# Waits of TensorE at the matmuls that need them, and thirteen opening matmuls less, in a scan with adapters behind it

## The chip, the cores and the metric

The kernel runs on one core of a Trainium2 chip. The metric is the device time of one execution in microseconds, the median of several runs. Profiles are taken from one further execution; their times count from the start of its span.

## The reference

```python
h = zeros((8, 128))
for t in range(6400):                     # for each of 8 sequences
    h = a[:, t] * h + b[:, t]             # a, b: (8, 6400, 128), f32
    x[:, t] = h
x = x.reshape(51200, 128)
logits = x @ w_gate                       # 128 -> 8 experts
top 2 of 8, softmax over the two: w
delta = sum over the two of w * ((x @ A[e]) @ B[e])    # rank 16
out = x + delta                           # (51200, 128), f32
```

The kernel reads a and b once (52.6 MB) and writes the output once (26.2 MB).

## The kernel before, in words

The 51,200 tokens are cut into 100 chunks of 512. Tokens lie on partitions when they are loaded (`a_tm`, `b_tm`, four slots of four chunks each) and have to stand along the free axis for the scan, so each chunk goes through these steps:

- Loads. `x` (a, four chunks, 1 MB) and `y` (b, two chunks, 512 KB) are issued by SyncE's queue (SP) and wait until TensorE has read the old contents of the slot.
- Transposes on TensorE (line 306, against `ident_f`) into PSUM. Chunks at the beginning and the end are done alone (`a`, `b`: four matmuls of 128x128). All others are fused (`f`, line 403): sixteen matmuls, in which eight of a's, for a chunk some way ahead, alternate with eight of b's, on the two halves of the rows. b goes to banks 1 and 2 in turn (`BANK_B`), which the scan frees; all other operations of TensorE take the six banks of `RING` in turn, which the copy out of the bank frees.
- a is copied to `a_st` by ScalarE (`a`, line 342); VectorE runs the scan (`s`, line 358) with a from SBUF and b from PSUM, and writes `xT`.
- `z` (line 455): up to three blocks of 128 tokens times the eight adapters' A and the gate, 136 columns each; ScalarE copies the result to `zl` (line 462).
- The gating of a group (six chunks in the middle, one or two at the ends), in small operations `1` to `8`, `p`, `q`, `r`, `u` on VectorE, GpSimd and ScalarE, lines 487 to 520.
- `m` (line 544): zl times gate, on GpSimd or VectorE; `t` (line 552): transposes of the product, for one or two chunks; a copy to `zwT` on ScalarE or VectorE (line 561).
- `d` (lines 579 and 580): for each of four blocks, the block of `xT` times the identity, then `zwT` times B on top of it. ScalarE copies to `outt` (`o`, line 587), SP stores (line 616), one or two chunks at a time.

Each engine does its operations in the order that the strings of `ORDER` spell, letter by letter (line 24 on). `Program.arrange` lays them out, `banks` gives the PSUM banks out in TensorE's order and adds a dependence on the copy that frees each, and `waits` walks through all five orders and finds which semaphore counts an operation has to wait for that its engine does not know of already. `run` (line 663) issues all waits of an operation ahead of its first instruction. The last instruction of an operation raises the engine's semaphore by one. SP's string mixes loads and stores in one order, so a store that waits holds back the loads behind it.

At the beginning `w` (line 262) transposes the identity into the last bank of the ring: `WARM` = 14 times, five before the first data, the others between the first chunks' operations. Nothing reads the results.

Of the kernel before, what the change touches and what calls it, by code (L numbers as in the profile page):

```python
# [58 lines left out]


class Op:
    __slots__ = ("i", "eng", "kind", "deps", "emit", "sem", "cnt", "clock", "dur", "alt", "lock", "size", "pos", "ring", "rows")


class Bank:


    __slots__ = ("n", "evac")


class Program:
# [4 lines left out]
    def __init__(self):  # L76
        self.ops = []
        self.at = 0.0

    def add(self, eng, kind, deps, emit, sem=None, dur=0.0, lock=False, alt=None, size=0, ring=None, rows=0):  # L80
# [8 lines left out]
        op.rows = rows  # L89
        self.ops.append(op)  # L90
        return op

# [18 lines left out]
    def banks(self, ring):  # L111

        turns = []
        for op in self.order["pe"]:
            if op.ring is not None:
                op.ring.n = ring[len(turns) % len(ring)]
                assert len(turns) < len(ring) - 1 or not any(o.kind == "w" for o in self.order["pe"][self.order["pe"].index(op) :])
                if len(turns) >= len(ring):
                    op.deps.append(turns[-len(ring)].evac)
                turns.append(op.ring)  # L120

    def waits(self):
        landed = {}
        out = {}
        known = {e: {} for e in self.ENGINES}
        at = {e: 0 for e in self.ENGINES}
        left = len(self.ops)
        while left:
            moved = False
            for e in self.ENGINES:  # L130
                while at[e] < len(self.order[e]):
                    op = self.order[e][at[e]]
                    if any(d.clock is None for d in op.deps):
                        break
                    k = known[e]
                    need = {}
                    for d in sorted(op.deps, key=lambda d: -d.i):
                        if d.sem is None and d.eng == e == "pe":
                            continue
                        key = d.eng if d.sem is None else d.sem  # L140
                        if k.get(key, 0) < d.cnt:
                            need[key] = max(need.get(key, 0), d.cnt)
                            for kk, v in d.clock.items():
                                k[kk] = max(k.get(kk, 0), v)
                            k[key] = max(k.get(key, 0), d.cnt)
# [12 lines left out]
def bass_associative_scan_2x2__then__mixture_of_adapters_kernel(  # L158
# [21 lines left out]
    span = {}  # L180
# [7 lines left out]
    with ExitStack() as stack:  # L188
# [41 lines left out]
        P = Program()  # L230
        eng = {}
# [4 lines left out]
        s_eng = {e: sem("s_" + e) for e in ("pe", "act", "dve", "pool")}  # L236
        s_dma = {}
# [23 lines left out]
        for k in range(WARM):  # L261
            w = P.add("pe", "w", [o_id], lambda: eng["pe"].transpose(ps[:, RING[-1], 0:128], ident_f[:, :], ident_f[:, :]),
                      dur=0.212)
# [7 lines left out]
        o_la, o_lb, place = {}, {}, [{}, {}]  # L271
# [114 lines left out]
        def front(c):  # L386
            P.at = c
            bb = Bank()
            bb.n = bank_b(c)
            sl, q, m, h = place[0][c]  # L390
            if m == 1:
                solo_a(c, 0)
            elif (c - h, 0) not in o_A:
                for p in (0, 2):
                    for g in (0, 1):
                        solo_a(c - h + p, g)
            deps, ts = turned(1, c, bb)
# [39 lines left out]
        def scanned(b):  # L437
            c0, m = span[b // 4]
            return o_sc[c0 + m - 1]
# [7 lines left out]
        def zlogits(b0, n):  # L447
            P.at = (b0 + n - 1) / 4
            bk = Bank()
            z0 = zpos[b0]  # L450
            assert n <= 3

            def zmm():
                for k in range(n):
                    last = eng["pe"].matmul(ps[:, bk.n, k * W : k * W + W], xblock(b0 + k), Awg_h)  # L455
                return last

            o = P.add("pe", "z", [scanned(b0 + n - 1), o_ch], zmm, dur=(0.059 if span[b0 // 4][1] == 1 else 0.062) * n, ring=bk)
            for k in range(n):
                reads(b0 + k, o)  # L460
            z = P.add("act", "z", [o] + [z_user[z0 + k] for k in range(n)],
                      lambda: eng["act"].copy(  # L462
                          zl[:, z0 : z0 + n, :].rearrange("p k w -> p (k w)"), ps[:, bk.n, 0 : n * W]),
                      dur=0.145 + 0.1172 * n)
            bk.evac = z
            for k in range(n):
                o_ze[b0 + k] = z
                z_user[z0 + k] = z
# [59 lines left out]
        def back(gi, c0, q0, n):  # L528
# [41 lines left out]
        def out_chunk(c, e_t):  # L570
# [9 lines left out]
                    last = eng["pe"].matmul(dst, zwT[:, w, k * 128 : k * 128 + 128], B_h, start=False, stop=True)  # L580
# [82 lines left out]
        def run(name, handle):  # L663
            eng[name] = handle
            for op in P.order[name]:
                for key, v in waits[op.i]:
                    handle.wait_ge(s_eng[key] if key in s_eng else s_dma[key], v)
# [18 lines left out]

        @block.tensor
        def _(pe):
            run("pe", pe)

        @block.scalar
        def _(act):
# [2 lines left out]
        @block.vector  # L695
        def _(dve):
            run("dve", dve)


class Unordered(Exception):  # L700
# [29 lines left out]
```

## Time and profile before

| | |
|---|---|
| Median of 3 runs | 203.28 us (203.12 to 203.54) |
| Profiled execution | 203.03 us, of which the span is 201.2 |
| Granted TensorE clock, mean | 0.987 |
| Busy: PE, DVE, ACT, POOL | 179.9, 177.1, 178.2, 127.4 us |
| DMA | 79.28 MB, mean 394 GB/s |
| Matmuls | 3150 |

PE is TensorE's matrix part, PEld its loading of weights, DVE VectorE, ACT ScalarE, POOL GpSimd, SP SyncE. The queue of an engine is marked with a q. L306 is line 306 of the kernel, the one before. "Issue" is time for which the profile shows no reason. Durations of TensorE's matmuls overlap: the distance of two starts tells the pace, not the duration.

### The profile page before, as it was taken

How to read it: one execution, taken by the hardware profiler on the slowest of the kernel's cores; microseconds unless marked ns; L12 is line 12 of the kernel's file. 1: busy time of each engine (PE TensorE's matmuls, PEld its weight loads, DVE VectorE, ACT ScalarE, POOL GpSimd, SP SyncE). 2: the span in 40 equal slices, each digit the busy share in tenths (PEclk: the TensorE clock that was granted, in tenths of full speed). 3: DMA queues.
4: the chain of work that ended last, by engine and by line, in shares of the span. 5: the costliest groups of instructions: out<-in, count | busy, mean ns of one | idle time of the engine just before them, and what ended most of it. 6: DMA issues, size and time to landing. Idle time of an engine off the chain costs nothing.

```text
span 201.2 us, 7662 instructions
## 1 busy us (share of the span) xinstructions
PE 179.9 (89%) x3150; PEld 164.3 (82%) x3150; DVE 177.1 (88%) x269; ACT 178.2 (89%) x384; POOL 127.4 (63%) x205
## 2 busy tenths in 40 slices
PE   4986788899989998999999999899999999898880
PEld 3975676788989998899999998789989898897760
DVE  0587689999989998999999999898999999999860
ACT  2376597999999999999999999899999999999970
POOL 1024006692797979785998697678788885865420
PEclk9999699999999999999999999999999999999998
DMA  6999999999999999999999999999999999998596
GB/s 189 396 410 414 414 410 412 416 421 396 419 415 419 409 411 423 410 423 406 419 418 405 418 415 415 416 415 414 422 410 411 415 407 404 418 360 346 234 357 226
DMA packets 21379, 79.28 MB, mean 394 GB/s; under 512 B 3424, under 2 KB 3552, under 8 KB 18400
## 3 DMA queue, kind: packets, MB, share of 16 engines
q1 hardware_dynamic: 19872, 78.39, 96.5%
q10 hardware_dynamic: 1472, 0.40, 0.9%
q8 instruction: 25, 0.41, 0.9%
q14 instruction: 10, 0.08, 0.1%
HBM read 52.56 MB, written 26.21 MB: 391 GB/s over the span
## 4 chain that ended last, share of the span: by engine, by line
PE 51%; DVE 17%; DMA 16%; ACT 5%; issue 4%; SPq 3%; POOL 2%; ACTq 0%
PE ps L306 20%; DMA b_tm<-in_b_dram 16%; DVE xT L358 10%; PE ps L455 10%; PE ps L579 8%; PE ps L552 7%; PE ps L580 6%; DVE zw L544 3%; ACT outt L587 3%; SPq L291 3%; ACT zl L462 1%; DVE zwT L561 1%; POOL g L518 1%; DVE L L492 1%; DVE k L490 0%
## 5 line engine op out<-in xcount | busy, mean ns | idle before, releaser
L358 DVE TENSOR_TENSOR_SCAN xT<-a_st,xT,ps 128x512 f16<-128x512 f32 x96 | 120.2, 1253 | 7.4 <-PE ps L306 5.3
L544 POOL TENSOR_TENSOR zw<-zl,g 128x512 f16<-128x512 f32 x82 | 85.9, 1069 | 9.9 <-PE ps L552 8.6
L306 PE MATMUL ps<-ident_f,a_tm 64*128 64x64 f32 (+1 forms) x768 | 66.3, 232 | 6.6 <-DVE xT L358 2.4
L462 ACT COPY zl<-ps 128x408 f32<-128x408 f32 (+1 forms) x138 | 67.9, 596 | 4.7 <-PE ps L455 4.5
L342 ACT COPY a_st<-ps 128x512 f32<-128x512 f32 x100 | 62.9, 691 | 7.3 <-PE ps L306 6.9
L306 PE MATMUL ps<-ident_f,b_tm 64*128 64x64 f32 (+1 forms) x768 | 66.0, 233 | 2.8 <-DMA b_tm<-in_b_dram 1.5
L306 PEld LDWEIGHTS ps<-ident_f,a_tm 64*128 64x128 f32 (+1 forms) x768 | 55.9, 141 | 13.0 <-issue 3.0
L587 ACT COPY outt<-ps 128x512 f32<-128x512 f32 x100 | 61.5, 691 | 2.9 <-PE ps L580 2.3
L306 PEld LDWEIGHTS ps<-ident_f,b_tm 64*128 64x128 f32 (+1 forms) x768 | 54.9, 141 | 4.4 <-issue 2.4
L579 PE MATMUL ps<-ident_h,xT 128*128 128x128 f16 x400 | 57.3, 231 | 0.6 <-ACT zwT L561 0.4
L580 PE MATMUL ps<-cst_h,zwT 128*128 128x128 f16 x400 | 55.7, 220 | 1.7 <-issue 1.7
L579 PEld LDWEIGHTS ps<-ident_h,xT 128*128 128x128 f16 x400 | 49.5, 142 | 3.9 <-ACT zwT L561 0.9
L580 PEld LDWEIGHTS ps<-cst_h,zwT 128*128 128x128 f16 x400 | 42.7, 107 | 1.1 <-issue 1.1
L455 PE MATMUL ps<-cst_h,xT 128*128 128x136 f16 x400 | 41.7, 232 | 1.3 <-DVE xT L358 0.9
L455 PEld LDWEIGHTS ps<-cst_h,xT 128*128 128x128 f16 x400 | 32.2, 145 | 4.2 <-DVE xT L358 1.4
L552 PE MATMUL ps<-ident_h,zw 128*128 128x128 f16 x400 | 30.8, 219 | 1.4 <-DVE k L490 0.6
L552 PEld LDWEIGHTS ps<-ident_h,zw 128*128 128x128 f16 x400 | 23.9, 98 | 3.3 <-ACT outt L587 0.8
L561 ACT COPY zwT<-ps 128x1024 f16<-128x1024 f16 (+1 forms) x21 | 21.7, 1033 | 0.0
L561 DVE COPY zwT<-ps 128x1024 f16<-128x1024 f16 (+1 forms) x31 | 20.3, 658 | 1.2 <-PE ps L552 1.2
L518 POOL TENSOR_TENSOR g<-k,w 128x192 f32<-128x192 f32 (+3 forms) x23 | 10.7, 467 | 11.4 <-DVE k L503 9.5
L498 POOL TENSOR_TENSOR dd<-m 128x24 f32<-128x24 f32 (+3 forms) x23 | 5.8, 251 | 16.5 <-DVE m L496 16.5
L501 POOL TENSOR_TENSOR dd<-m 128x24 f32<-128x24 f32 (+3 forms) x23 | 6.0, 259 | 15.1 <-DVE m L496 15.0
(23 smaller groups left out, 90.2 us busy)
## 6 DMA issues: line engine op xcount, KB each, us to landing
a_tm<-in_a_dram SPq DMA_DIRECT2D x23, 1024.0 KB, 16.4
b_tm<-in_b_dram SPq DMA_DIRECT2D x46, 512.0 KB, 16.8
out_dram<-outt SPq DMA_DIRECT2D x46, 512.0 KB, 14.4
a_tm<-in_a_dram SPq DMA_DIRECT2D x8, 256.0 KB, 9.7
out_dram<-outt SPq DMA_DIRECT2D x8, 256.0 KB, 5.2
b_tm<-in_b_dram SPq DMA_DIRECT2D x7, 256.0 KB, 11.8
b_tm<-in_b_dram ACTq DMA_DIRECT2D x1, 256.0 KB, 3.6
cst_f<-in_moe_A_dram ACTq DMA_DIRECT2D x1, 64.0 KB, 4.3
```

The costliest lines, as they stand in the source:

```text
L306: return [lambda k=k: eng["pe"].transpose(dv(k), src[r, 8 * g + k, :], ident_f[r, r]) for k in range(n)]
L342: lambda: eng["act"].copy(dst, src()), dur=AE[0 if m == 1 else 1])
L358: last = eng["dve"].tensor_tensor_scan(out=xT[:, xb, s0:s1], data0=a_st[:, c % NA, s0:s1], data1=ps[:, bk, s0:s1], initial=init, op0=ALU.m ...
L455: last = eng["pe"].matmul(ps[:, bk.n, k * W : k * W + W], xblock(b0 + k), Awg_h)
L462: lambda: eng["act"].copy(zl[:, z0 : z0 + n, :].rearrange("p k w -> p (k w)"), ps[:, bk.n, 0 : n * W]),
L518: lambda: eng["pool"].tensor_tensor(out=gg, in0=kk2, in1=bc(u2), op=ALU.mult), dur=pd)
L544: lambda me=me, wv=wv, zv=zv, gv=gv: eng[me].tensor_tensor(out=wv, in0=zv, in1=gv, op=ALU.mult),
L552: last = eng["pe"].transpose(ps[:, bt.n, :].bitcast(F16)[:, k * 128 : k * 128 + 128], zw[:, w + k // 4, k % 4, :], ident_h[:, :])
L561: f = (lambda: eng["act"].copy(dst, src())) if te == "act" else (lambda: eng["dve"].tensor_copy(dst, src()))
L579: eng["pe"].matmul(dst, xblock(b0 + k), ident_h[:, :], start=True, stop=False)
L580: last = eng["pe"].matmul(dst, zwT[:, w, k * 128 : k * 128 + 128], B_h, start=False, stop=True)
L587: lambda: eng["act"].copy(outt[:, p0 : p0 + 4, :].rearrange("p k d -> p (k d)"), ps[:, bo.n, :]), dur=0.6)
```

## The change

`WARM` goes from 14 to 1, and the thirteen letters `w` go from TensorE's string; nothing else in any order changes. All else concerns where TensorE waits. An operation now knows the number of its matmuls (`mm`) and which of its dependences only a later matmul needs (`late`: a place and the dependences). In `f` that is the second matmul, for all but a's load and the ring's bank; in `d` the second, for the copy `zwT` and for B; in `t` the fifth, for the product of the second chunk. Then `lend` goes through TensorE's order: where an operation would still wait for two or more semaphores ahead of its first matmul, one of them, a DMA's if there is one, is waited for at the last matmul of the operation before it, as long as the wait does not depend on that operation itself and the orders still run through. A wrapper around the engine counts the matmuls of an operation and puts each wait ahead of the one it belongs to. In the built programs 501 matmuls of the new one wait for one semaphore and 46 for two; before, 216 waited for one, 105 for two, 22 for three and 19 for four.

```diff
-WARM = 14
+WARM = 1
...
-        "wwwwwbawwabwzzwwwwbwwazzbaaaazzaztffffzztzfdzzffzzfdfzfzzzffzzftzzffdzfdzzftzfzfzdfdzfzzzfzzfttzzffd"
+        "wbaabzzbazzbaaaazzaztffffzztzfdzzffzzfdfzfzzzffzzftzzffdzfdzzftzfzfzdfdzfzzzfzzfttzzffd"
...
                 if len(turns) >= len(ring):
-                    op.deps.append(turns[-len(ring)].evac)
+                    evac = turns[-len(ring)].evac
+                    op.deps.append(evac)
+                    op.late = (op.late[0], [d for d in op.late[1] if d is not evac])
...
+    def lend(self):
+
+        waits = self.waits()
+        pe = self.order["pe"]
+        for prev, op in zip(pe, pe[1:]):
+            need = dict(waits[op.i][0][1])
+            last = prev.mm - 1
+            if len(need) < 2 or last < 1 or prev.tail or last == prev.late[0]:
+                continue
+            for key in sorted(need, key=lambda k: k in self.ENGINES):
+                moved = [d for d in op.deps if (d.eng if d.sem is None else d.sem) == key and d is not prev]
+                if any(self.reaches(d, prev) for d in moved):
+                    continue
+                prev.tail = moved
+                try:
+                    self.waits()
+                    break
+                except AssertionError:
+                    prev.tail = []
...
-                    need = {}
-                    for d in sorted(op.deps, key=lambda d: -d.i):
...
-                    out[op.i] = list(need.items())
+                    out[op.i] = []
+                    for place, part in ((0, [d for d in op.deps if d not in op.late[1]]), op.late, (op.mm - 1, op.tail)):
+                        need = {}
+                        for d in sorted(part, key=lambda d: -d.i):
...
+                        out[op.i].append((place, list(need.items())))
...
-                o = P.add("pe", "f", deps + deps2, each(ts2, ts), dur=FUSED[2], lock=True, ring=ba)
+                o = P.add("pe", "f", deps + deps2, each(ts2, ts), dur=FUSED[2], lock=True, ring=ba, mm=16, late=(1, [d for d in deps if d is not o_id]))
...
-            o = P.add("pe", "z", [scanned(b0 + n - 1), o_ch], zmm, dur=(0.059 if span[b0 // 4][1] == 1 else 0.062) * n, ring=bk)
+            o = P.add("pe", "z", [scanned(b0 + n - 1), o_ch], zmm, dur=(0.059 if span[b0 // 4][1] == 1 else 0.062) * n, ring=bk, mm=n)
...
-            o_t = P.add("pe", "t", o_mu + [o_ih], tr, dur=0.224 * n, ring=bt)
+            o_t = P.add("pe", "t", o_mu + [o_ih], tr, dur=0.224 * n, ring=bt, mm=4 * n, late=(4, o_mu[1:]))
...
-            o_D[c] = P.add("pe", "d", [e_t, o_cB], delta, dur=0.448 if span[c][1] == 1 else 0.48, ring=bo)
+            o_D[c] = P.add("pe", "d", [e_t, o_cB], delta, dur=0.448 if span[c][1] == 1 else 0.48, ring=bo, mm=8, late=(1, [e_t, o_cB]))
...
         P.banks(RING)
+        P.lend()
         waits = P.waits()
...
             for op in P.order[name]:
-                for key, v in waits[op.i]:
-                    handle.wait_ge(s_eng[key] if key in s_eng else s_dma[key], v)
+                if name == "pe":
+                    handle.at(waits[op.i], lambda key, v: pe_wait(s_eng[key] if key in s_eng else s_dma[key], v))
+                else:
+                    for _, needs in waits[op.i]:
...
+class Matmuls:
+    def __init__(self, pe):
+        self.pe, self.n, self.places = pe, 0, []
+
+    def at(self, places, wait):
+        self.n, self.places, self.wait = 0, places, wait
+
+    def ready(self):
+        for place, needs in self.places:
+            if place == self.n:
+                for key, v in needs:
+                    self.wait(key, v)
+        self.n += 1
+
+    def transpose(self, *args):
+        self.ready()
+        return self.pe.transpose(*args)
+
+    def matmul(self, *args, **kwargs):
+        self.ready()
+        return self.pe.matmul(*args, **kwargs)
```

More of the change, by code (lines that the diff above doesn't have):

```diff
@@ L61 @@
 class Op:
-    __slots__ = ("i", "eng", "kind", "deps", "emit", "sem", "cnt", "clock", "dur", "alt", "lock", "size", "pos", "ring", "rows")
+    __slots__ = ("i", "eng", "kind", "deps", "emit", "sem", "cnt", "clock", "dur", "alt", "lock", "size", "pos", "ring", "rows", "mm", "late", "tail")
 class Bank:
@@ L78, in __init__, with add @@
         self.at = 0.0
-    def add(self, eng, kind, deps, emit, sem=None, dur=0.0, lock=False, alt=None, size=0, ring=None, rows=0):
+    def add(self, eng, kind, deps, emit, sem=None, dur=0.0, lock=False, alt=None, size=0, ring=None, rows=0, mm=1, late=(0, ())):
         op = Op()
@@ L88, in add @@
         op.ring = ring
-        op.rows = rows
+        op.rows, op.mm, op.tail = rows, mm, []
+        op.late = (late[0], [x for d in late[1] for x in (d if isinstance(d, list) else [d])])
         self.ops.append(op)
@@ L118, in banks, with reaches @@
                 if len(turns) >= len(ring):
-                    op.deps.append(turns[-len(ring)].evac)
+                    evac = turns[-len(ring)].evac
+                    op.deps.append(evac)
+                    op.late = (op.late[0], [d for d in op.late[1] if d is not evac])
                 turns.append(op.ring)
+    def lend(self):
[16 more added lines that the diff above has]
+                    prev.tail = []
+    def reaches(self, op, target):
+        todo, seen = [op], set()
+        place = {o.i: (e, k) for e in self.ENGINES for k, o in enumerate(self.order[e])}
+        while todo:
+            o = todo.pop()
+            if o is target:
+                return True
+            if o.i in seen or o.clock is None:
+                continue
+            seen.add(o.i)
+            if o.clock.get("pe", 0) >= target.cnt:
+                return True
+        return False
     def waits(self):
@@ L124, in waits @@
         out = {}
+        for op in self.ops:
+            op.clock = None
+            if op.sem is not None:
+                op.cnt = 0
         known = {e: {} for e in self.ENGINES}
@@ L132, in waits @@
                     op = self.order[e][at[e]]
-                    if any(d.clock is None for d in op.deps):
+                    if any(d.clock is None for d in op.deps + op.tail):
                         break
                     k = known[e]
-                    need = {}
-                    for d in sorted(op.deps, key=lambda d: -d.i):
[L138 to L145, printed above, removed]
-                    out[op.i] = list(need.items())
+                    out[op.i] = []
+                    for place, part in ((0, [d for d in op.deps if d not in op.late[1]]), op.late, (op.mm - 1, op.tail)):
+                        need = {}
+                        for d in sorted(part, key=lambda d: -d.i):
+                            if d.sem is None and d.eng == e == "pe":
+                                continue
+                            key = d.eng if d.sem is None else d.sem
+                            if k.get(key, 0) < d.cnt:
+                                need[key] = max(need.get(key, 0), d.cnt)
+                                for kk, v in d.clock.items():
+                                    k[kk] = max(k.get(kk, 0), v)
+                                k[key] = max(k.get(key, 0), d.cnt)
+                        out[op.i].append((place, list(need.items())))
                     op.clock = dict(k)
@@ L660, in bass_associative_scan_2x2__then__mixture_of_adapters_kernel, with run @@
         P.banks(RING)
+        P.lend()
         waits = P.waits()
-        def run(name, handle):
+        def run(name, handle, pe_wait=None):
             eng[name] = handle
             for op in P.order[name]:
-                for key, v in waits[op.i]:
-                    handle.wait_ge(s_eng[key] if key in s_eng else s_dma[key], v)
+                if name == "pe":
[3 more added lines that the diff above has]
+                        for key, v in needs:
+                            handle.wait_ge(s_eng[key] if key in s_eng else s_dma[key], v)
                 inst = op.emit()
@@ L688, in _ @@
         def _(pe):
-            run("pe", pe)
+            pe_wait = pe.wait_ge
+            run("pe", Matmuls(pe), pe_wait)
         @block.scalar
@@ L697, in _ @@
             run("dve", dve)
+class Matmuls:
[6 more added lines that the diff above has]
+            if place == self.n:
+                for key, v in needs:
+                    self.wait(key, v)
[6 more added lines that the diff above has]
+        return self.pe.matmul(*args, **kwargs)
 class Unordered(Exception):
```

## The prediction

> **What bounds the kernel now.** I read the page first (busy times, DMA, clock), then busy time by stage, then the chain that ended last.
>
> ```profile
> span 201.2 us, 7662 instructions
> PE 179.9 (89%) x3150; PEld 164.3 (82%) x3150; DVE 177.1 (88%) x269; ACT 178.2 (89%) x384; POOL 127.4 (63%) x205
> ...
> 137.00:160.00 23.00, 22.54 (x431) 20.74 (x431) 21.61 (x31) 22.69 (x49) 18.90 (x25) 1.00 1.02 414
> 160.00:176.00 16.00, 14.98 (x239) 14.20 (x236) 15.86 (x22) 15.49 (x35) 11.79 (x19) 1.00 1.04 410
> 176.00:199.30 23.30, 18.08 (x266) 16.28 (x263) 17.79 (x47) 18.52 (x40) 9.49 (x27) 1.00 0.84 329
> ```
>
> Each stage row gives its length, the busy time of PE, PEld, DVE, ACT and POOL, the granted clock, the DMA share and GB/s. Three engines are close to full everywhere, so busy shares decide nothing. The DMA column does: until 176 us all sixteen DMA engines are occupied (share 1.02 to 1.04, over 400 GB/s); from 176 to 199.3 the share is 0.84, which leaves 0.16 x 23.3 = 3.7 us of free DMA time. Before 176 the kernel cannot move its bytes faster; only after it can an earlier engine shorten anything.
>
> ```profile
> 6.83 15.16 DMA b_tm<-in_b_dram
> ...
> 141.31 17.86 DMA b_tm<-in_b_dram
> 159.22 1.80 PE ps L306 x36
> ...
> 161.42 1.27 DVE xT L358
> ...
> 170.46 1.20 DVE xT L358
> 171.65 0.14 issue
> 171.79 0.63 PE ps L306 x4
> ...
> 192.94 1.34 DVE zw L544 x2
> 194.27 0.05 issue
> 194.32 0.40 PE ps L552 x4
> ...
> 195.33 1.17 ACT outt L587 x2
> ```
>
> This is the chain in order of time (start, length, what). A load of b issued at 141.31 lands 17.86 us later, at 159.2, and TensorE starts on it at 159.22. TensorE was already waiting for loads there:
>
> ```profile
> PE ps L306 <- DMA a_tm<-in_a_dram: 0.3, 1, 0.3
> ```
>
> That is the only TensorE idle time in the waits of 137 to 160 us, and a load ends it. So whatever TensorE gains between 22 and 137 us is handed back as a longer wait for loads: they come out of one saturated queue whose order the SP string fixes. After 161.42 the chain is the scans on VectorE (15.86 of 16 us busy), at 171.79 four microseconds of TensorE, and at the end the gating of the last chunks, ScalarE's copies and two short TensorE operations.
>
> **The change part by part.** The profiled execution took 203.03 us, span 201.2 and 1.8 around it; the median of the runs is 203.28, 0.25 above. I work in differences, taken off the median.
>
> *Fewer waiting instructions.* [...]
>
> ```profile
> L667 PEldq EVENT_SEMAPHORE  x165: 51/51/1167, 6.9 to 194.7; - x165
> L667 PEldq EVENT_SEMAPHORE  x26: 51/51/51, 160.0 to 194.7; - x26
> ```
>
> The rows are one line's instructions (minimum, median and maximum in ns), of the whole run and from 160 us. In the built programs the number falls from 166 to 47, and among the matmuls that run after 160 us in this trace from 26 to 2. The upper bound of what this is worth is 119 x 51 ns = 6.1 us in all and 24 x 51 ns = 1.2 us after 160. The lower bound is zero, since the queue runs ahead of the array. Where it shows is in the fused transposes:
>
> ```profile
> 60.62 0.27 PE L306 MATMUL ps<-ident_f,a_tm 64*128 64x64 f32 x1
> 60.62 0.27 PE L306 MATMUL ps<-ident_f,b_tm 64*128 64x64 f32 x1
> 60.73 0.22 PE L306 MATMUL ps<-ident_f,a_tm 64*128 64x64 f32 x1
> ...
> 60.80 0.22 PE L306 MATMUL ps<-ident_f,a_tm 64*128 64x64 f32 x1
> ...
> 60.86 0.22 PE L306 MATMUL ps<-ident_f,a_tm 64*128 64x64 f32 x1
> ```
>
> Pairs follow each other every 0.06 us, but the pair behind the one with several waits comes after 0.11: 0.05 us lost per such operation; 74 of the 90 fused operations have such an instruction ahead of them, and some 40 pairs in this trace come so late: 2 us. All of it lies before 160 us, under the loads, so it counts zero; if the loads did not cover it, it would be 2 us. After 160 the 24 removed instructions stand mostly ahead of f16 matmuls. Between 171.7 and 175.7, where TensorE itself is the chain, there are five. I count those five in full: 5 x 0.05 = 0.25 us (ends 0 and 1.2).
>
> *Late waits.* Of the sixteen matmuls of `f` only the second on now waits for b's load and for the bank that the scan frees; `d` does its first matmul before it waits for the copy; `t` of two chunks starts on the first. For `f` TensorE stands at the second matmul instead of the first: nothing. The last `d` closes the chain behind the copy of the last `t`: one matmul less after the wait.
>
> ```profile
> 195.24 0.25 PE L579 MATMUL ps<-ident_h,xT 128*128 128x128 f16 x1
> 195.32 0.22 PE L580 MATMUL ps<-cst_h,zwT 128*128 128x128 f16 x1
> ```
>
> The second starts 0.08 us after the first, and 0.08 is the gain; twice at most, since the `d` before it is released in the same way. The later start of `t` on its second half can give 4 x 0.06 us per operation, but the last two `t` are of one chunk and have no second half: zero.
>
> *Lent waits.* 76 waits move to the last matmul of the operation before. Behind it queue that operation's own signal and whatever ScalarE or VectorE copies out of its bank. For each I set the time at which this trace's semaphore reached the awaited count against the start of the lending matmul: seven are reached after it, 1.06 us late at 25.96 and at most 0.4 elsewhere, the largest from 160 us on 0.07. The late one at 25.96 is this wait, which now ends the fused operation ahead of it:
>
> ```profile
> PE ps L455 <- DVE xT L358: 0.9, 1, 0.9
> ```
>
> It comes from the waits of 22 to 60 us, where the loads cover it; uncovered it would cost up to that 0.9 us. The cost is bounded by zero and by the rival below; I take zero.
>
> *The opening.* Thirteen transposes of the identity go.
>
> ```profile
> 4.34 1.12 PE L306 MATMUL ps<-ident_f,b_tm 128*128 128x128 f32 x4 [1.48 <-DMA b_tm<-in_b_dram]
> ...
> 8.60 0.60 PE L262 MATMUL ps<-ident_f 128*128 128x128 f32 x4
> 9.04 0.60 PE L306 MATMUL ps<-ident_f,b_tm 128*128 128x128 f32 x4
> ...
> 18.50:21.90 3.40, 1.85 (x37) 1.51 (x32) 3.40 (x5) 2.40 (x6) 0.00 (x0) 1.00 1.01 401
> 22.00:25.30 3.30, 3.27 (x40) 2.96 (x42) 1.53 (x4) 1.06 (x3) 0.37 (x2) 0.50 1.02 418
> PE ps L306 <- DMA b_tm<-in_b_dram: 1.1, 1, 1.1
> ```
>
> Four transposes take 1.12 us at 4.34 and 0.60 at 9.04, so TensorE comes up to speed near 8.5 us; after a stretch in which it was busy 1.85 of 3.4 us the clock falls to 0.50 for the next 3.3. With the spare matmuls gone, the stretch from 4.3 to 8.3 still holds sixteen transposes of data; the next one thins out and may be granted half. That costs up to 1.7 us of TensorE (half of 3.4), against 1.1 us that it waits for a load before 22.03 (last row, waits of 15 to 23 us). What is left falls under 6.83 + 15.16 of the chain's DMA: zero, with the rest in a rival. [...]
>
> Sum: 0.25 + 0.08 = 0.33, with the second `d` 0.4: 203.28 - 0.4 = 202.9 us.
>
> **The rivals.** *Nothing (203.2).* The queue in TensorE runs ahead, so that five fewer instructions at 171.7 give nothing, and VectorE takes up the rest. For it: VectorE is busy 15.86 of 16 us. Against it is a wait on the chain itself, which ends at 171.79 and after whose release another 0.14 us pass (the chain at 171.65):
>
> ```profile
> PE ps L306 <- DVE xT L358: 0.8, 1, 0.8
> ```
>
> *More (201.9).* All 24 instructions after 160 us count (1.2 us), and earlier copies send stores into the 3.7 us of free DMA time. Against it: ACT and VectorE close most of the waits there.
>
> *Lent waits turn round (204.0).* Once TensorE runs a little earlier, a lending matmul stands until the awaited engine is done, its own operation is signalled that much later, and the copy behind it starts late. A release costs 0.14 us to the first matmul (171.65). Fifteen waits are lent after 160 us; if five bind on the chain that is 0.7 us. It decides where the awaited count comes after the lending matmul; in this trace that is so for two of the fifteen, by 0.05 and 0.07 us, with one more within 0.05 before it.
>
> [...]
>
> **How the numbers follow.** A measurement of this kernel can tell about 0.2% (0.4 us) from no change. Small gain at the tail, 0.1 to 0.8 us: 0.50, of which I give 0.28 beyond 0.4 us. More: 0.17. Nothing: 0.10. Lent waits: 0.13. Cold opening: 0.10. So faster 0.28 + 0.17 = 0.45, same 0.22 + 0.10 = 0.32, slower 0.23. The range runs from 201.7, the 1.2 us and a little refilled DMA, to 204.4, short of the middle of the cold opening.
>
> **What would show it.** Right: the extra waiting instructions fall to some 46 rows of 51 ns; the second pair of a fused operation follows after 0.06 us; a load still ends TensorE's waits before 160 us, and the b load of 159.2 lands within 0.5 us of it; the chain from there is as long as before or shorter by under 0.8 us. Wrong: that landing moves by more than 1 us (the opening reached DMA), copies of ScalarE late behind lending matmuls after 160 us, or a chain in which TensorE carries the last 40 us.

## The result

The changed kernel takes 202.19 us (median of six runs, 202.12 to 202.45); the kernel before, measured beside it, 203.19 us (202.81 to 203.54). The ratio is 0.9951, 95% interval [0.9941, 0.9961]: faster by 0.5%, 1.0 us. Measured once more (`after_again` below), it took 201.99 us against 203.18. Ratios here and below leave out executions that are more than 1.5% above the fastest of the same kernel, and where single executions are long they differ from the quotient of the medians.

### The profile after

In the changed kernel all matmuls have the wrapper's lines: L768 the transposes (L306 before and, for `t`, L552), L772 the others (L455, L579, L580). The other lines are 44 higher: L402 the scan, L588 `m`, L605 the copy to `zwT`, L631 that to `outt`; L712 are TensorE's extra waits (L667). The head of its page, with the row of DMA queue q8, whose kind is "instruction" (packets, MB, share of 16 engines; the other row of that kind, q14, is the same in all runs):

```profile
span 200.4 us, 7516 instructions
PE 179.6 (90%) x3137; PEld 163.5 (82%) x3137; DVE 178.1 (89%) x269; ACT 178.0 (89%) x384; POOL 127.9 (64%) x205
q8 instruction: 24, 0.39, 0.8%
```

The profiled execution took 202.23 us. Busy time by stage (length, PE, PEld, DVE, ACT, POOL with their instructions, clock, DMA share, GB/s) hardly differs from before:

```profile
137.00:160.00 23.00, 22.50 (x419) 20.49 (x417) 22.16 (x31) 22.14 (x48) 19.46 (x26) 1.00 1.02 414
160.00:176.00 16.00, 15.06 (x243) 14.30 (x240) 15.66 (x22) 15.59 (x35) 11.71 (x19) 1.00 1.03 410
176.00:199.30 23.30, 18.19 (x269) 16.38 (x265) 18.05 (x48) 18.64 (x40) 9.71 (x27) 0.98 0.84 331
```

The chain that ended last, from the load of b at 141.25 on:

```profile
141.25 18.16 DMA b_tm<-in_b_dram
159.45 1.79 PE ps L768 x35
161.24 0.40 PE ps L772 x6
161.64 1.27 DVE xT L402
...
170.72 1.20 DVE xT L402
171.96 1.10 PE ps L768 x12
...
176.03 0.67 DVE zwT L605
...
193.18 1.34 DVE zw L588 x2
194.57 0.40 PE ps L768 x4
194.96 0.52 PE ps L772 x8
195.50 1.17 ACT outt L631 x2
```

It is the same chain, and none of it is earlier. The load lands at 141.25 + 18.16 = 159.41 (159.17 before), TensorE starts on it at 159.45 (159.22), ScalarE's last copy ends at 195.50 + 1.17 = 196.67 (195.33 + 1.17 = 196.50). All compute ends 0.17 us *later* than before, and yet the span is 0.8 us shorter. (In the profile of `after_again` the load lands at 159.18 and the last copy ends at 196.48, both as before: the 0.17 belongs to this one execution.) So the gain lies behind the last copy: 201.2 - 196.50 = 4.7 us from there to the end of the span before, 200.4 - 196.67 = 3.7 us after. All that is left there is the last stores. SP's issues of `outt` from 194 us on, first of the kernel before, then of the changed one:

```profile
DMA to landing us min/median/max: 4.1/4.2/5.0
```

```profile
DMA to landing us min/median/max: 3.1/3.6/4.2
```

The rows give the minimum, the median and the maximum. The last store, issued at 196.58 us before and at 196.70 after, lands after 4.1 us before and after 3.2 us now. What else was in the DMA queues then? In the kernel before, the row of queue q8 on the page and, under it, in the window from 192 to 194 us:

```profile
q8 instruction: 25, 0.41, 0.9%
...
q8 instruction: 1, 0.02, 4.7%
```

In the changed kernel, 187 to 189 us, the last one that it has:

```profile
q8 instruction: 1, 0.02, 3.0%
```

These packets have 16,384 bytes each, and in the kernel before they start from the 305th of TensorE's recorded instructions, at 19.35 us, to the 6,376th, at 192.13: 25 in all, 183 to 377 instructions apart, 253 on average. The runs below, which change TensorE's number of instructions and nothing on the other engines, have 24, 25 or 26 of them (24 with 6,324 recorded, 25 with 6,469, 26 with 6,596), and from this they are read as TensorE's program being fetched. 4.7% of 2 us on sixteen engines is 1.5 us. Before, the 25th packet starts at 192.13, amid the last stores, which SP issues from 189.7 us on. The changed program has 145 instructions fewer on TensorE (6,324 recorded instead of 6,469: 26 of thirteen matmuls with their weight loads, 119 waiting ones; the expectations below count two more in each kernel); its 24th packet starts at 187.66, ahead of those stores, and it has no 25th.

### The profile page after: what moved, and what is told of

Its sections match the earlier page's. It is cut to its first block, busy times and chain, and to the rows that moved or that the text cites. A ratio compares the mean times of both kernels' runs of the same rounds, so it can differ in the third digit from the quotient of the medians.

```text
span 200.4 us, 7516 instructions
## 1 busy us (share of the span) xinstructions
PE 179.6 (90%) x3137; PEld 163.5 (82%) x3137; DVE 178.1 (89%) x269; ACT 178.0 (89%) x384; POOL 127.9 (64%) x205
## 4 chain that ended last, share of the span: by engine, by line
PE 38%; DMA 25%; DVE 15%; ACT 13%; SPq 3%; issue 2%; POOL 2%; ACTq 0%
DMA b_tm<-in_b_dram 25%; PE ps L768 20%; PE ps L772 18%; DVE xT L402 8%; ACT zl L506 4%; ACT outt L631 4%; DVE zw L588 4%; ACT a_st L386 3%; SPq L335 3%; ACT zwT L605 1%; DVE L L536 1%; DVE zwT L605 1%; DVE k L534 1%; POOL g L562 1%; DVE m L540 0%
## 5 line engine op out<-in xcount | busy, mean ns | idle before, releaser
L402 DVE TENSOR_TENSOR_SCAN xT<-a_st,xT,ps 128x512 f16<-128x512 f32 x96 | 120.3, 1253 | 7.6 <-PE ps L768 5.6
L588 POOL TENSOR_TENSOR zw<-zl,g 128x512 f16<-128x512 f32 x82 | 85.8, 1068 | 11.6 <-PE ps L768 10.1
L506 ACT COPY zl<-ps 128x408 f32<-128x408 f32 (+1 forms) x138 | 70.7, 631 | 4.8 <-PE ps L772 4.8
L768 PE MATMUL ps<-ident_f,b_tm 64*128 64x64 f32 (+1 forms) x768 | 65.3, 231 | 8.8 <-DVE xT L402 4.6
L386 ACT COPY a_st<-ps 128x512 f32<-128x512 f32 x100 | 64.6, 721 | 8.3 <-PE ps L768 8.3
L768 PE MATMUL ps<-ident_f,a_tm 64*128 64x64 f32 (+1 forms) x768 | 67.5, 232 | 1.0 <-ACT a_st L386 0.7
L631 ACT COPY outt<-ps 128x512 f32<-128x512 f32 x100 | 62.7, 719 | 2.3 <-PE ps L772 1.3
L768 PEld LDWEIGHTS ps<-ident_f,b_tm 64*128 64x128 f32 (+1 forms) x768 | 54.3, 140 | 11.2 <-DMA b_tm<-in_b_dram 4.8
L768 PEld LDWEIGHTS ps<-ident_f,a_tm 64*128 64x128 f32 (+1 forms) x768 | 56.2, 140 | 6.5 <-ACT a_st L386 1.0
L772 PE MATMUL ps<-cst_h,zwT 128*128 128x128 f16 x400 | 56.2, 221 | 1.5 <-ACT zwT L605 0.8
L772 PE MATMUL ps<-ident_h,xT 128*128 128x128 f16 x400 | 57.4, 231 | 0.0
L772 PEld LDWEIGHTS ps<-ident_h,xT 128*128 128x128 f16 x400 | 49.7, 142 | 1.6
L772 PEld LDWEIGHTS ps<-cst_h,zwT 128*128 128x128 f16 x400 | 42.5, 107 | 2.8 <-ACT zwT L605 1.1
L772 PE MATMUL ps<-cst_h,xT 128*128 128x136 f16 x400 | 41.7, 233 | 1.8 <-DMA a_tm<-in_a_dram 0.9
L772 PEld LDWEIGHTS ps<-cst_h,xT 128*128 128x128 f16 x400 | 32.1, 145 | 4.8 <-DVE xT L402 1.2
L768 PE MATMUL ps<-ident_h,zw 128*128 128x128 f16 x400 | 31.7, 222 | 1.8 <-DVE zw L588 0.7
L768 PEld LDWEIGHTS ps<-ident_h,zw 128*128 128x128 f16 x400 | 24.5, 99 | 4.1 <-DVE zw L588 1.2
L605 ACT COPY zwT<-ps 128x1024 f16<-128x1024 f16 (+1 forms) x21 | 22.3, 1060 | 0.0
L605 DVE COPY zwT<-ps 128x1024 f16<-128x1024 f16 (+1 forms) x31 | 20.3, 657 | 0.2 <-PE ps L768 0.2
```

What stands on the lines that cost most here:

```text
L386: lambda: eng["act"].copy(dst, src()), dur=AE[0 if m == 1 else 1])
L402: last = eng["dve"].tensor_tensor_scan(out=xT[:, xb, s0:s1], data0=a_st[:, c % NA, s0:s1], data1=ps[:, bk, s0:s1], initial=init, op0=ALU.m ...
L506: lambda: eng["act"].copy(zl[:, z0 : z0 + n, :].rearrange("p k w -> p (k w)"), ps[:, bk.n, 0 : n * W]),
L588: lambda me=me, wv=wv, zv=zv, gv=gv: eng[me].tensor_tensor(out=wv, in0=zv, in1=gv, op=ALU.mult),
L605: f = (lambda: eng["act"].copy(dst, src())) if te == "act" else (lambda: eng["dve"].tensor_copy(dst, src()))
L631: lambda: eng["act"].copy(outt[:, p0 : p0 + 4, :].rearrange("p k d -> p (k d)"), ps[:, bo.n, :]), dur=0.6)
```

## The experiments

Three theories of the 1.0 us. **F**, fetch: only where the instruction packets fall among the last stores counts, so the *number* of TensorE's instructions decides. **W**, waits: the moved waits shorten TensorE's own path. **O**, opening: the thirteen matmuls do it. The padding in the kernels below is a wait for a count of GpSimd that is meant to have been reached long ago, and does nothing else. Kernels 1 to 4 ran on one chip (before there: 203.1 us), 5 to 7 on another (203.18), 8 to 10 on that one later (203.06); 11 and 12 are one execution each, on the first.

**1. `pad_before`: the kernel before and 127 waiting instructions more**, spread over its `z`, `t` and `d`.

```diff
+PAD = 165
...
+        pads = [o.i for o in P.order["pe"][60:] if o.kind in "zdt" and waits[o.i]][:PAD]
...
+                if name == "pe" and op.i in pads:
+                    handle.wait_ge(s_eng["pool"], 1)
```

> The kernel before, all its waits and its opening kept, with 127 waiting instructions more on TensorE, spread over z, t and d operations from the opening to the middle of the run; each waits for a count that GpSimd reached long ago. [...] Theory W (waits): fewer waiting instructions and later waits shorten the last 40 us; more of them then give 203.2 or up to 204. Theory O (opening): the earlier first chunks are what helps; then nothing changes here, 203.2.

Measured: 206.33 us, ratio 1.0162 [1.0143, 1.0182]. By F the 25th packet, with 127 instructions more ahead of it, comes before the last stores, and the 1.0 us is saved; the time missed that by 4 us. Its page and the end of its chain:

```profile
span 205.0 us, 7789 instructions
q8 instruction: 26, 0.43, 0.8%
```

```profile
199.02 1.17 ACT outt L588 x2
```

The last copy ends at 200.19, 3.7 us later than before: the padding itself delayed TensorE, which reached the b load of 159.1 only at 163.0. 3.7 us by 127 are 0.03 us an instruction on average. And the longer program fetched a 26th packet, at 200.66, once more among the stores: 205.0 - 200.19 = 4.8 us from the copy to the end. The run prices waiting instructions in places where TensorE has work; it does not decide on F.

**2. `pad_after`: the changed kernel and 145 waiting instructions more**, back to 6,469 recorded, in the same manner (`[50:]`, `PAD = 145`).

> The changed kernel with 145 such waiting instructions more on TensorE, so that it has as many instructions as the kernel before. F: the last instruction packet comes back to some 95 instructions before the end, near 192 us, among the last stores: about 203.2 us, 1.0 slower than the changed kernel. W: the late and lent waits are kept and most of the added instructions lie ahead of f16 matmuls before 160 us: 202.2 to 202.5. O: 202.2.

Measured: 204.5 us (203.1 to 206.54), ratio 1.0053 [1.0028, 1.0077], longer than any of the theories had it. The same flaw: compute ends at 198.15 in its profile. The packet starts at 192.03, but here 6.1 us ahead of the last copy's end, and the span ends 3.75 us behind it. Slower for the padding's own time, then, and no proof for F.

**3. `open_only`: the kernel before with one opening matmul.**

```diff
-WARM = 14
+WARM = 1
-        "wwwwwbawwabwzzwwwwbwwazzbaaaazz...
+        "wbaabzzbazzbaaaazz...
```

> The kernel before with the thirteen opening matmuls removed and nothing else: 26 TensorE instructions fewer (a matmul and its weight load each). F: the last instruction packet comes with some 70 instructions left instead of 93, near 193 us, still among the last stores: 203.0 to 203.4 us. W: 203.2. O: 202.2 to 202.5.

Measured: 203.06 us (202.33 to 203.38), ratio 0.9998 [0.9988, 1.0008]. The opening alone is worth nothing; O falls. With 26 instructions fewer the 25th packet starts later, at 194.13, still among the stores.

**4. `waits_only`: the changed kernel with fourteen opening matmuls** (the same two lines the other way), and **8. `waits_only_2`**, the same once more.

> The changed kernel with all fourteen opening matmuls and the old order of the opening. F: some 240 TensorE instructions are left at the last instruction packet, near 186 us: 202.2 us. W: 202.2. O: 203.2.

> The changed waits with the fourteen opening matmuls, once more (6352 instructions on TensorE). Its twelve times lay between 201.97 and 203.06, while its profile, at 202.04, shows the last instruction packet at 185.23 us and none among the last stores. [...] Theory O (the opening matmuls cost something once the waits are moved): one group near 202.7.

Measured: 202.71 us (201.97 to 203.06), ratio 0.9979 [0.9966, 0.9992], and 202.61 us (201.76 to 203.27), 0.9978 [0.9958, 0.9998]. The medians lie between the two kernels because the executions form two groups: of 24 spans, 14 lie in 199.8 to 200.4 us and 10 in 201.1 to 201.5. F had 202.2 for the first and missed it; the second was forecast with the first known. Both profiles have a short span; of 11 and 12 below, one has a long one.

The time of an execution is longer than its span, by 1.75 to 1.95 us in every execution of the kernel before on record. Of the 14 with a short span here, seven have more, 2.05 to 2.77 us. One of them is the profile of `waits_only_2`: 202.59 us with a span of 200.0. Its page counts 24 packets, but from 200 to 203 us, behind the last instruction, its queue q8 has one more, at 201.87:

```profile
q8 instruction: 1, 0.02, 2.0%
```

So the 25th packet can also come behind the span. That it is what made the time longer there, and in the other six, fits but is not shown.

**5. `after_again`: the changed kernel, beside the next two.**

> The changed kernel itself, beside the next two on one chip: 202.2 us by every theory; the reference for them.

Measured: 201.99 us (201.84 to 204.08), ratio 0.9964 [0.9939, 0.9989].

**6. `open_pad_after`: the changed kernel and 60 waiting instructions at places where TensorE stands idle**, 40 ahead of the first transpose of b and 20 ahead of the first operation that waits for the load of 22 us (two waits make one instruction: 120 more waits took the page from 7,516 to 7,576).

```diff
+PADS = 80, 40
...
+        first = next(o.i for o in P.order["pe"] if o.kind == "b")
+        later = next(o.i for o in P.order["pe"] if any(key == "lb2_0" for _, part in waits[o.i] for key, v in part))
+        pads = {first: PADS[0], later: PADS[1]}
...
+                for k in range(pads.get(op.i, 0) if name == "pe" else 0):
+                    pe_wait(s_eng["pool"], 1)
```

> The changed kernel with 60 waiting instructions more on TensorE, all put where it idles anyway: 40 ahead of the first data (idle from 2.0 to 4.3 us), 20 ahead of the fused operation that waits for a load until 21.9 us. F (fetch): with 60 more the twenty-fifth instruction packet, which the changed kernel never reaches, comes again, with about 10 TensorE instructions left, near 195.5 us, on the very last stores: 202.8 to 203.2 us. W (waits) and O (opening): 60 x 0.05 us in idle time cost nothing, 202.2 to 202.3.

Measured: 203.95 us (202.72 to 205.76), ratio 1.0044 [1.0015, 1.0072]. The direction is F's, the size larger. In the profile the 25th packet is back, at 195.90, and the stores take a median of 4.8 us instead of 3.6. But the last copy also ends 0.7 us later, at 197.37. The padding was not quite free: the first load has landed at 4.26 us and TensorE begins at 5.87 (4.33 without). The granted clock was also 0.50 for 6.8 us from 20.23 on in this execution. Which of the two made the copy late was not separated, so the time of this kernel is no measure of the packet alone; the 4.6 us behind the copy are.

```profile
0.74 3.52 DMA b_tm<-in_b_dram
4.26 1.61 issue
5.87 1.96 PE ps L775 x8
```

**7. `open_pad_before`: the kernel before and 66 waiting instructions in such places**, 30, 16 and 20. The 25th packet should come earlier by them, out of the stores. If F holds, *adding* instructions makes the kernel before faster.

```diff
+PADS = 60, 32, 40
...
+        pads = {first: PADS[0], mid: PADS[1], later: PADS[2]}
...
+                for k in range(pads.get(op.i, 0) if name == "pe" else 0):
+                    handle.wait_ge(s_eng["pool"], 1)
```

> The kernel before with 66 waiting instructions more, all put where TensorE idles: 30 ahead of the first data, 16 and 20 ahead of the fused operations that stand until 18 and 22 us. F: the last instruction packet comes with some 155 instructions left instead of 93, near 190 us, in the gap of DMA between two stores: 202.2 to 202.6 us, faster although instructions are added. W and O: 203.1 to 203.4.

Measured: 202.05 us (201.81 to 204.44), ratio 0.9963 [0.9941, 0.9984], as fast as the changed kernel and a little below F's range. Its page, its queue q8 from 189 to 191 us, the end of its chain and the landing of its stores from 194 us on:

```profile
span 200.2 us, 7728 instructions
q8 instruction: 25, 0.41, 0.8%
```

```profile
q8 instruction: 1, 0.02, 2.9%
```

```profile
195.29 1.17 ACT outt L588 x2
```

```profile
DMA to landing us min/median/max: 3.1/3.5/4.1
```

As many packets as before, the last at 189.94; the copies end at 196.46, as before (196.50); the stores land like those of the changed kernel. All old waits and the old opening are in this kernel, so W and O have no part in its gain. The gain of the change can be had without the change.

**9. `waits_warm4`: the changed waits, four opening matmuls** (6,330 recorded instructions).

> The changed waits with four opening matmuls, all ahead of the first data: twenty instructions fewer than with fourteen, 6332. F: too few for the 25th packet, as in the changed kernel: nearly all times within 201.8 to 202.3, median 202.0 to 202.1. O: the matmuls among the first chunks are gone, and of the 0.7 us between 202.7 and 202.0 most is gone too, 202.1 to 202.3; the kernel of the next run decides between the two.

Measured: 201.97 us, ratio 0.9954 [0.9937, 0.997]. Two of ten executions were long. The one of 203.0 has no profile; the other is the profiled one (202.73), and it is long for another reason: 24 packets, the stores fast, but the last copy at 197.22, after a stretch of lower granted clock (0.93) between 137 and 160 us, after which TensorE comes to the load that lands at 159.10 only at 159.83.

```profile
137.00:160.00 23.00, 22.36 (x397) 20.62 (x397) 19.72 (x28) 20.51 (x45) 17.28 (x24) 0.93 1.02 415
```

**10. `pad26_after`: the changed kernel and 26 waiting instructions ahead of the first transpose**, 6,350 recorded, as in `waits_only`.

> The changed kernel with one opening matmul and 26 waiting instructions ahead of the first transpose of b, where TensorE stands idle for the first load: 6352 instructions as with fourteen opening matmuls, none of them a matmul. F: times in two groups again, 202.0 and 203.0, median 202.3 to 202.8. O: 202.0 as the changed kernel. If the 26 waits delay the first transposes (26 x 0.05 us = 1.3 us against a wait of some 1.5 us there), at most 0.3 us more.

Measured: 201.91 us, ratio 0.9951 [0.9932, 0.9969]; all six spans in 200.0 to 200.3. F's two groups did not appear; one of the six (202.68) has 2.38 us more than its span, like those of `waits_only` above. By its time the run speaks for O: with fourteen opening matmuls the same number of instructions took 202.6 to 202.7. By the profiles it does not: the last copy ends at 196.36 here and at 196.22 to 196.40 in the four profiles with fourteen, so the opening costs compute nothing, and what it changes lies behind the copy. With 6,350 recorded instructions the number alone does not say when a 25th packet comes, among the stores, behind the span or not at all; what else does stays open.

**11 and 12. `waits_look_1`, `waits_look_2`: `waits_only` again, one execution each, for a long one.**

> The changed waits with fourteen opening matmuls, one more execution with a profile, to catch one of its long executions (10 of 24 had a span of 201.1 to 201.5 us, the others 199.8 to 200.4). If it is a long one, F: a 25th instruction packet among the stores after 190 us, the last store 4 us from issue to landing, the chain's end at 196.4 as in the short ones. Another cause (a lower clock, or a late load, at a place that the loads no longer cover): 24 packets, the last store 3.1 us from issue to landing, the chain's end about 1 us later. If it is a short one (span below 200.5), it tells nothing.

> The same kernel and the same question as the run before: one more chance to catch a long execution. F: a 25th packet and a slow last store; other cause: 24 packets and a late chain's end.

The first took 203.13 us, the second 201.72: the same program on the same chip. Page, end of the chain and landing of the stores from 194 us on, of the long one:

```profile
span 201.3 us, 7542 instructions
q8 instruction: 25, 0.41, 0.8%
```

```profile
195.23 1.17 ACT outt L631 x2
```

```profile
DMA to landing us min/median/max: 4.3/4.8/5.4
```

And of the short one:

```profile
span 199.9 us, 7542 instructions
q8 instruction: 24, 0.39, 0.8%
```

```profile
195.05 1.17 ACT outt L631 x2
```

```profile
DMA to landing us min/median/max: 3.0/3.1/4.1
```

Compute ends within 0.18 us in both. The long one fetched the 25th packet, at 196.88, when all but the last of its recorded TensorE instructions had started; the short one had its last at 185.07. The span is 1.4 us longer, 1.2 of it behind the last copy. This is the cleanest evidence: not an instruction of the program differs.

The runs together, by their profiles:

| kernel | end of last copy, us | last packet, us before that end | end of span, us after it |
|---|---|---|---|
| after | 196.67 | 9.0 | 3.7 |
| after_again | 196.48 | 9.1 | 3.7 |
| waits_warm4 | 197.22 | 9.0 | 3.7 |
| waits_look_2 | 196.22 | 11.2 | 3.7 |
| waits_only | 196.40 | 11.2 | 3.7 |
| waits_only_2 | 196.34 | 11.1 (and one behind the span) | 3.7 |
| pad26_after | 196.36 | 11.3 | 3.7 |
| open_pad_before | 196.46 | 6.5 | 3.7 |
| pad_after | 198.15 | 6.1 | 3.75 |
| **before** | 196.50 | 4.4 | 4.7 |
| open_only | 196.80 | 2.7 | 4.6 |
| open_pad_after | 197.37 | 1.5 | 4.6 |
| pad_before | 200.19 | -0.5 | 4.8 |
| waits_look_1 | 196.40 | -0.5 | 4.9 |

Where the last packet before the span's end starts 6.1 us or more ahead of the last copy's end, the span ends 3.7 or 3.75 us behind that copy; where it starts from 4.4 us ahead to 0.5 behind, 4.6 to 4.9 us, which is 0.9 to 1.2 more.

## Why the prediction was right, and where it was not

The forecast was 202.9, the time is 202.19: faster, as forecast, and inside the range. The bound and the cover were read rightly; the sum that made it faster was not the cause, and the cause was in none of the cases. Of the 1.0 us the mechanism that was forecast shows 0.08, at the late `d`: that the gain was over twice the 0.4 us of the forecast, and still inside the range, was luck.

**The cover of the loads before 160 us: right.** TensorE did gain, and the gain was gone by 160 us. Busy time by stage, first before, then after; the count behind the first busy time is of matmuls:

```profile
0.00:22.00 22.00, 15.33 (x174) 13.55 (x174) 12.79 (x24) 12.48 (x28) 4.41 (x19) 1.00 0.94 356
22.00:60.00 38.00, 34.39 (x616) 30.39 (x617) 34.33 (x49) 33.87 (x74) 21.21 (x34) 0.96 1.02 413
60.00:100.00 40.00, 39.24 (x762) 36.52 (x760) 38.85 (x53) 39.66 (x86) 32.02 (x44) 1.00 1.02 415
100.00:137.00 37.00, 35.30 (x682) 32.62 (x682) 35.84 (x50) 35.54 (x79) 29.60 (x42) 1.00 1.02 415
```

```profile
0.00:22.00 22.00, 13.67 (x164) 11.54 (x166) 12.78 (x24) 12.75 (x28) 4.40 (x19) 1.00 0.96 356
22.00:60.00 38.00, 35.74 (x666) 31.73 (x667) 36.48 (x50) 35.13 (x79) 22.86 (x38) 1.00 1.02 412
60.00:100.00 40.00, 39.95 (x774) 37.35 (x772) 39.41 (x55) 40.00 (x90) 33.34 (x45) 1.00 1.02 415
100.00:137.00 37.00, 34.45 (x626) 31.65 (x624) 33.57 (x45) 33.74 (x72) 26.40 (x36) 0.95 1.02 415
```

Without the thirteen that are gone, by 100 us the changed kernel has done 164 + 666 + 774 = 1604 against 174 - 13 + 616 + 762 = 1539: 65 matmuls ahead, some 3 us at the pace of 60 to 100 us. By 137 us the lead is 9, by 160 us it is gone. Part of this is the clock and not the change. The 0.96 before is one stretch of 3.4 us at 0.50 from 21.92 us on, which this execution of the changed kernel does not have; its own, of the same length, comes at 119.85, in the row with 0.95. `after_again`, the same kernel, has its stretch at 22.03, as before:

```profile
22.00:60.00 38.00, 35.68 (x633) 31.60 (x635) 34.92 (x48) 33.69 (x76) 21.40 (x35) 0.96 1.02 413
```

It has done 162 + 633 + 783 = 1578 by 100 us, 39 matmuls or 2 us ahead, with the clock alike. That much is the change's. It too is gone by 160 us, with no slow stretch between; of the 2.9 us that TensorE waits there from 60 to 160 us, loads end 2.5. In the first execution its waits from 60 to 137 us name loads as well (0.8 us more go to a scan), where before they named none:

```profile
PE ps L772 <- DMA a_tm<-in_a_dram: 0.9, 1, 0.9
PE ps L768 <- DMA b_tm<-in_b_dram: 0.8, 1, 0.8
```

The load of b lands 0.24 us later than before, within the 0.5 that the prediction allowed. In this kernel 2 us of TensorE were worth nothing: the DMA share is 1.02 in the rows from 22 to 160 us in both kernels, and the last load landed no earlier for them.

**Fewer waiting instructions: the count right, the 0.25 us not there.** The rows fell to 46, two of them from 160 us on. The changed kernel's line of waits, the whole run and then from 160 us:

```profile
L712 PEldq EVENT_SEMAPHORE  x46: 51/51/51, 7.0 to 169.5; - x46
L712 PEldq EVENT_SEMAPHORE  x2: 51/51/51, 167.5 to 169.5; - x2
```

Before there were 165, which is what the counts of waits give if one such instruction holds up to two of them: 105 + 22 + 2 x 19. So in this kernel one such instruction stands for one wait or for two.

The stretch that should have become shorter by five of them runs from the end of the scan ahead of it, 171.65 before and 171.91 after, to the copy behind it, which starts at 176.03 after and before with this row of the chain:

```profile
175.77 0.67 DVE zwT L561
```

That is 4.12 us in both. In the profiles of `before`, `open_only` and `open_pad_before`, with the old waits, and of eight executions with the new ones (all but the two whose padding delayed the last copy), it is 4.12 or 4.13. The term is zero, the lower end that the prediction named. The queue did run ahead of the array there: the waiting instruction at 172.15 us in the kernel before stands, by the program's order, ahead of a `z` whose first matmul starts at 173.18. Waiting instructions can cost something (0.03 us each in `pad_before`); whether that lead is why these five do not is not shown.

**The fused pairs: wrong, at no price.** The second pair was to follow after 0.06 us. It still follows after 0.11 (TensorE's timeline of the changed kernel, a's row of the first two pairs of an `f`):

```profile
91.64 0.27 PE L768 MATMUL ps<-ident_f,a_tm 64*128 64x64 f32 x1
...
91.75 0.22 PE L768 MATMUL ps<-ident_f,a_tm 64*128 64x64 f32 x1
```

It is so in some 60 of the 90 fused operations, as before, where the prediction counted some 40. With 46 extra waiting instructions left in the whole program, such an instruction cannot be what makes all of these pairs late; what does, the wait at the second matmul perhaps, was not separated. The 2 us that the prediction put there under the loads did not come from there, and where TensorE's lead of 2 us came from is open.

**The late `d`: right.** From the last `t` to the last copy: 195.33 - 194.32 = 1.01 us before, 195.50 - 194.57 = 0.93 after, the 0.08 predicted. It is 1.01 us in the three profiles with the old waits and 0.93 or 0.94 in the eight with the new ones. Once, not twice: the stretch ahead of it, from 175.77 to 194.32 us before, is as long as ever, 18.55 and 18.54 us. From TensorE's start on the load to the last copy's end the chain is 196.67 - 159.45 = 37.22 us instead of 196.50 - 159.22 = 37.28. So the whole sum of 0.33 to 0.4 measured 0.06 to 0.08.

**The rivals.** *Nothing* was right for compute and wrong for the time. *More* gave a time near the measured one, 201.9, by another way: it had earlier copies send stores into free DMA time, and the copies did not come earlier. *Lent waits turn round*: from 160 us on no lent wait costs the chain anything that shows in its 37.22 us. *Cold opening*: the granted clock is 1.00 in the rows of the profile up to 100 us, and the load of b moved by 0.24 us; `open_only` shows the opening at nothing. No run shows the loss that the forecast's 0.10 and its end at 204.4 us rest on; what the runs showed in its place is 203.06 us for `open_only` against 203.1 for the kernel before, and 203.31 in its profiled execution, where the clock was 0.82 up to 22 us. The dip to 0.50 near 22 us, from which the 1.7 us for the opening were estimated, comes and goes between executions of one program: `after_again` has it (0.96 in its row above), the first execution of the changed kernel has not (1.00).

**The missed step.** The prediction took what lies behind the chain's last copy as fixed: 203.03 us as a span of 201.2 and 1.8, the span as a chain up to the last copy and whatever the stores then take. It never asked what was in those 4.7 us. The row "q8 instruction: 25" stood on the page, and the window of the last stores would have shown one of its packets there, at 192.13 us; with 145 instructions fewer on TensorE that packet was gone (24 instead of 25, the last at 187.66). At 1.0 us it was the largest term of the change, and the sum had it at nothing.

## What to carry to other kernels

Read the last stretch of the DMA queues as carefully as the last stretch of the engines: with an instruction packet among the last stores the span was 0.9 to 1.2 us longer here, and changes in the number of instructions took it out of them (145 fewer, or 66 more) or put it there (60 more in the changed kernel). A gain or loss of that size after an edit to instruction counts proves nothing for the edit's own reason until a kernel with the same edit and other padding has run; 66 idle instructions in a place of idle time gave all that this change gave. And a gain on an engine that waits for a saturated queue later on was no gain here, though it was 2 us half way. Before such a lead is put down to an edit, compare executions in which the clock is alike: 65 matmuls of lead were 39 when both had their stretch of 3.4 us at half clock.

## What was not expected of the hardware

- Packets of queue q8, kind "instruction", of 16,384 bytes each, are moved while the kernel runs, 25 in the kernel before and 24 in the changed one, one for some 250 recorded instructions of TensorE, each taking 0.9 to 1.5 us. With one among the last stores the span ends 0.9 to 1.2 us later behind the last copy (4.6 to 4.9 us instead of 3.7). By what way it makes the stores late is not shown; the profile does not tell the DMA engines apart.
- With 6,350 recorded instructions the same program sometimes has one packet more: ten of 24 executions of `waits_only` were long, and the one profiled later had 25 packets instead of 24. In another, the 25th came 1.8 us behind the end of the span.
- Waiting instructions of 51 ns each, for counts meant to be long met, cost TensorE 0.03 us each on average (127 of them, 3.7 us in `pad_before`); of the five that went behind the scan that ends at 171.65 us, nothing shows (4.12 us in both kernels).
- The granted clock fell to 0.50 for 3.4 us at 22.03 us in one execution of the changed kernel (`after_again`) and at 119.85 us in another (`after`): the program alone does not settle when.
